# One launch of attention, a dense layer and routed experts: the first pair's keys and queries in two parts, and the experts' partial products added on VectorE

## The chip, the cores and the metric

The kernel runs on one core of one Trainium2 chip, in one launch. Its metric is the device time of the launch in microseconds (us). Before the change three runs took 764.28, 765.04 and 766.53 us; the median is 765.04. The engines are called as in the profile: PE (TensorE, matrix products; PEld its weight loads), DVE (VectorE), ACT (ScalarE), POOL (GpSimd) and SP (the engine that issues most DMAs here).

## What is computed

```python
# q, k, v: 4 batches x 8 heads x 576 positions x 64
scores = q @ k.T / 8, where block(i) >= block(j) (blocks of 64 positions), else -1e9
attn   = softmax(scores) @ v                       # -> x: 2304 tokens x 512
g      = x @ w_in;  x = max(0.01 * g, g) @ w_out   # 512 -> 2048 -> 512, all tokens
do     = x @ w_skip > 0                            # the others keep x
e      = argmax(x[do] @ w_gate), p = its softmax   # one of 8 experts for a token
out    = x + p * (relu(x @ w1[e]) @ w2[e])         # 512 -> 1024 -> 512
```

All data are 32-bit floats. A plain 32-bit product on PE (scores, expert units) is recorded as two instructions, so the profile counts twice the products of the program. In the dense layer and the first expert the operands are split in a high and a low half, and three products are made of them.

## The kernel before, in words

**Attention** goes through 16 pairs of heads. For a pair, `load` issues the DMAs of keys (`kn`), queries (`qn`) and values (`vn`) in natural layout; `prep` transposes keys and queries on PE (L110, and L160 for the first pair), ACT copies the keys to `kT` (L149), DVE and ACT each scale one head's queries into a block-diagonal operand (L170, L168; both are called `wbt` in the rows, since that is the memory they lie in). `s_steps` makes the scores of nine blocks of 64 queries, both heads in one product (L182): 64 columns for block 0, 128 for block 1, up to 576. For every block DVE takes the maximum (L192, `stat`), ACT the exponential with its sum (L193), POOL multiplies by the reciprocal (L201); then PE transposes the weights (L288) and multiplies by the values (L345). Later pairs make the scores of two blocks at a time in another form, whose mask lies in constant operands that `constants` writes once (L85 zeroes, L88 entries; tiles `wbt` and `qc`). PE reads the first of them at 88.5 us.

**The dense layer** is L526 on PE. A quarter of its first product runs between the attention steps; the rest follows, 12 chunks of 128 columns for each of 6 parts of 384 tokens. In a chunk PE makes `ph` (12 products of 384 columns), ACT and DVE make the leaky maximum `u` (L516; L517 on DVE, which lets PE reuse the bank), and PE adds 9 products of 512 columns to `acc`. DVE adds the finished sums to the tokens (L902).

**Routing.** When a part of tokens is finished, its steps wait in a list `rq`, and one is taken per chunk. For four of the six parts DVE makes the logits: nine instructions of 128x512 for a tile of 128 tokens, one step per tile (L748, `xlast`; each has a short instruction that reads the accumulator). Their place among the `u` is the scheduler's.

**Experts.** The first expert runs as full tiles. What is left is done in units: five `Groups` of up to 3, 3, 3, 1 and 1 groups of 32 tokens, one `Half` of 64, one `Full` of 128. For a group, four products that use 32 columns of PE each stand side by side. `second_product` (L1283) gives four partial sums of 32x512, one in each quarter of a bank `pp`; ACT or DVE copies them (L1394, L1358), PE adds them by a product with a matrix of ones and zeros (`py`, L1399, L1362), and DVE adds gate times result to the tokens (L1291), which POOL scatters (L1292). POOL's gather and the transposes of the next unit (L1259) and its first product (L1269, L1274) are put between.

What is written out by hand has a due time (`steps` returns pairs of time and step), and a list scheduler orders the instructions of each engine; `pin` keeps an instruction where it is written. SP issues its DMAs in its own order.

Of the kernel before, what the change touches and what calls it, by code (L numbers as in the profile page):

```python
# [10 lines left out]
F32 = mybir.dt.float32  # L11
# [16 lines left out]
class Attention:  # L28
# [50 lines left out]
    def constants(self, i):  # L79

        nc, nt, o = self.nc, self.nt, self.operands[i]
        for t, c0, val, eng in (([o["kc"][:, h] for h in range(2)], 64, self.MASK, nc.vector), (o["qc"], 0, 1.0, nc.gpsimd)):
            for h in range(2):
# [4 lines left out]
                nc.vector.tensor_scalar(out=b, in0=row, scalar1=val, scalar2=None, op0=ALU.mult)  # L88

    def load(self, p, which):  # L90
# [8 lines left out]
        for t, src in todo:  # L99
            queue = nc.scalar if p == 0 and src is self.q else nc.sync  # L100
            for j in range(2):
                queue.dma_start(t[:, 0:n, j], src[b, h0 + j, 0 : n * 128].rearrange("(t p) d -> p t d", p=128))
            queue.dma_start(t[0:64, n], src[b, h0 : h0 + 2, n * 128 : S].rearrange("h p d -> p h d"))
# [36 lines left out]
    def prep(self, p, nat):  # L140
# [9 lines left out]

        def s_q():
            if p:
                parts = [(self.transposes(qn), 0, S)]
            else:
                f = qn.rearrange("p t h d -> p t (h d)")
                parts = []
                for i0, i1 in ((0, 512), (512, S)):
                    pt = self.ps.tile([128, 512], F32, name="pq", tag="mm", bufs=2)
                    for t in range(i0 // 128, -(-i1 // 128)):
                        nc.tensor.transpose(pt[:, 128 * t - i0 : 128 * t - i0 + 128], f[:, t], self.ident)  # L160
                    parts.append((pt[:, 0 : i1 - i0], i0, i1))
            sc = self.D ** -0.5
            for pt, i0, i1 in parts:
                for h in range(2):
                    r = slice(64 * h, 64 * h + 64)
                    o, i_ = qd[r, i0 // 64 : i1 // 64, r], pt[r].rearrange("p (i c) -> p i c", c=64)
                    if h:
                        nc.scalar.activation(out=o, in_=i_, func=AF.Copy, scale=sc)  # L168
                    else:
                        nc.vector.tensor_scalar(out=o, in0=i_, scalar1=sc, scalar2=None, op0=ALU.mult)  # L170

        return st, [s_k, s_q]
# [182 lines left out]
    def steps(self, dst, lag, second):  # L355
# [16 lines left out]
        out.append((0.2, lambda: self.load(0, "v")))  # L372
        for p in range(pairs):
            t = 2 * p
            st = lambda p=p: sts[p]["st"]
            for i in range(2):
                out.append((t - ((0.9, 0.6), (1.4, 1.0))[p > self.SPLIT][i] if p else -1, lambda p=p, i=i: prep(p, i)))
            if p + 1 < pairs:
                out.append((t + lag if p else 0.6, lambda p=p: self.load(p + 1, "v")))
# [18 lines left out]
def attention_moe_kernel(  # L398
# [89 lines left out]
    def weights_a(parts, times):  # L488
# [22 lines left out]
        return [(-0.5, lambda j=j: fetch(j)) for j in range(2)] + [  # L511
# [213 lines left out]
    def routing_steps(n, x2):  # L725
# [16 lines left out]
        def logits(t):  # L742

            if t == 0:
                box["L"] = s3("lg", 1 + E)
            for j in range(1 + E):
# [106 lines left out]
        return [keep] + [lambda t=t: (logits_last if late else logits)(t) for t in range(TB)] + [route, place_all, put]  # L853
# [234 lines left out]
    for i in range(len(seq) + lag):  # L1088
# [8 lines left out]
        for _ in range(1 if i < len(seq) - NFB else 2):  # L1097
            if rq:
                rq.pop(0)()
# [177 lines left out]
    def second_product(pp, w, h, m):  # L1277

        s = 128 // m
        n = NF2 // s  # L1280
        for i in range(n):
            for j in range(s):
                pin(nc.tensor.matmul(pp[j * m : j * m + m], h[:, i * 128 + j * m : i * 128 + j * m + m], w[1][j * n + i], start=(i == 0), stop=(i == n - 1)))  # L1283

    def end_tile(y, lx, n=128):
        yo = M3.tile([128, 512], F32, name="yo")
# [226 lines left out]
```

## Time and profile before

| what | value |
|---|---|
| median of three runs | 765.04 us |
| the profiled execution | 765.64 us |
| its span, first to last instruction | 763.80 us |
| outside the span | 1.84 us |
| PE busy | 730.6 us (96%) |
| DVE, ACT, POOL busy | 460.4, 354.9, 319.2 us |
| PE idle and waiting for the first keys | 5.0 us |

The span is what the timeline shows, from 0 to 763.80; the launch's time has 1.84 us more, which no view resolves. A busy share is an average over stages: DVE is busy 60% of the span, but 49.90 of the 50 us from 450 to 500. The attention lasts to about 310 us, the dense layer to about 640 us, the units of the experts run from 682 us on.

### The profile page before, as it was taken

How to read it: one execution, taken by the hardware profiler on the slowest of the kernel's cores; microseconds unless marked ns; L12 is line 12 of the kernel's file. 1: busy time of each engine (PE TensorE's matmuls, PEld its weight loads, DVE VectorE, ACT ScalarE, POOL GpSimd, SP SyncE). 2: the span in 40 equal slices, each digit the busy share in tenths (PEclk: the TensorE clock that was granted, in tenths of full speed). 3: DMA queues.
4: the chain of work that ended last, by engine and by line, in shares of the span. 5: the costliest groups of instructions: out<-in, count | busy, mean ns of one | idle time of the engine just before them, and what ended most of it. 6: DMA issues, size and time to landing. Idle time of an engine off the chain costs nothing.

```text
span 763.8 us, 12641 instructions
## 1 busy us (share of the span) xinstructions
PE 730.6 (96%) x4454; PEld 593.1 (78%) x4455; DVE 460.4 (60%) x1067; ACT 354.9 (46%) x824; POOL 319.2 (42%) x429
## 2 busy tenths in 40 slices
PE   5999899999999999999999999999999998999995
PEld 4666778788888788899999998879899976875333
DVE  5888887764668646666773499988821365221211
ACT  4786887775788746555452222222223251222110
POOL 4656683454335436454442342545431543210111
PEclk9999999999999999999999999999999999999998
DMA  8545644522330214732223457112302221999900
GB/s 183 136 116 133 181 103 113 144 65 73 90 77 17 95 58 148 272 100 81 98 83 111 123 150 251 56 43 84 125 0 83 57 96 32 301 399 397 353 25 24
DMA packets 101109, 96.92 MB, mean 127 GB/s; under 512 B 69198, under 2 KB 72270, under 8 KB 101042
## 3 DMA queue, kind: packets, MB, share of 16 engines
q1 hardware_dynamic: 92578, 82.28, 34.5%
q0 software_dynamic: 7264, 13.50, 6.1%
q8 instruction: 36, 0.59, 0.3%
q10 hardware_dynamic: 1200, 0.30, 0.2%
q14 instruction: 31, 0.25, 0.1%
HBM read 74.38 MB, written 21.98 MB: 126 GB/s over the span
## 4 chain that ended last, share of the span: by engine, by line
PE 64%; DVE 21%; ACT 7%; DMA 3%; issue 2%; POOL 1%; SPq 0%; POOLq 0%; ACTq 0%; DVEq 0%
PE ph L526 18%; PE acc L526 12%; DVE xlast L748 9%; PE pv L345 4%; PE po L526 3%; PE ph L1269 3%; PE pp L1283 3%; PE pt L288 3%; PE py L1004 2%; PE sp L229 2%; PE ph L1004 2%; ACT P L193 2%; PE sp L182 2%; DVE stat L192 2%; PE big L110 1%
## 5 line engine op out<-in xcount | busy, mean ns | idle before, releaser
L526 PE MATMUL ph<-xT,wbt 128*128 128x384 f32 x864 | 167.2, 338 | 3.9 <-DVE u L517 2.1
L526 PEld LDWEIGHTS ph<-xT,wbt 128*128 128x128 f32 x864 | 151.8, 188 | 13.5 <-DVE u L517 3.9
L518 POOL TENSOR_TENSOR gl<-u,gh 128x384 fp32r<-128x384 f32 x72 | 80.5, 1119 | 144.5 <-ACT gh L517 140.8
L526 PE MATMUL acc<-wbt,gh 128*128 128x512 f32 x432 | 132.2, 393 | 0.0
L201 POOL TENSOR_SCALAR P<-P,stat 128x256 f32<-128x256 f32 (+4 forms) x144 | 80.0, 573 | 89.5 <-DVE stat L199 73.3
L517 ACT CAST gh<-u 128x384 fp32r<-128x384 f32 x72 | 37.0, 514 | 121.2 <-DVE u L517 49.6
L526 PEld LDWEIGHTS acc<-wbt,gh 128*128 128x128 f32 x432 | 79.7, 188 | 12.0
L517 DVE TENSOR_TENSOR u<-ph,u 128x384 f32<-128x384 f32 x72 | 39.7, 551 | 71.4 <-ACT u L516 71.3
L526 PE MATMUL acc<-wbt,gl 128*128 128x512 f32 x216 | 82.2, 395 | 0.0
L516 ACT ACTIVATE u<-ph 128x384 f32<-128x384 f32 x72 | 35.3, 490 | 61.3 <-PE ph L526 58.2
L288 PE MATMUL pt<-ident,P 128*128 128x128 f32 x400 | 58.2, 275 | 4.4 <-ACT P L193 1.8
L192 DVE TENSOR_REDUCE stat<-sp 128x1 f32<-128x384 f32 (+7 forms) x88 | 45.9, 527 | 25.1 <-PE sp L229 12.8
L288 PEld LDWEIGHTS pt<-ident,P 128*128 128x128 f32 x400 | 47.0, 140 | 16.5 <-ACT P L193 5.4
L193 ACT ACTIVATE P<-sp,stat 128x384 f32<-128x384 f32 (+7 forms) x88 | 49.8, 567 | 20.2 <-DVE stat L192 18.6
L526 PE MATMUL ph<-xT,wia 128*128 128x384 f32 x288 | 57.6, 344 | 0.6 <-ACT xT L350 0.5
L473 POOL TENSOR_TENSOR cv<-cv,cv 128x512 int32<-128x512 int32 x32 | 43.7, 1366 | 33.7 <-DVE cv L472 26.9
L526 PE MATMUL po<-woa,gA 128*128 128x512 f32 x216 | 55.4, 399 | 0.0
L748 DVE CUSTOM_DVE_ANT_0 xlast<-x,raw 128x512 f32<-128x512 f32 x72 | 55.1, 804 | 0.0
L526 PEld LDWEIGHTS ph<-xT,wia 128*128 128x128 f32 x288 | 49.4, 188 | 2.3 <-ACT xT L350 0.7
L345 PE MATMUL pv<-ph,vn 128*64 128x320 f32 (+4 forms) x448 | 49.6, 370 | 0.4 <-ACT P L242 0.3
L526 PEld LDWEIGHTS acc<-wbt,gl 128*128 128x128 f32 x216 | 40.4, 188 | 8.5
L345 PEld LDWEIGHTS pv<-ph,vn 128*64 128x64 f32 x448 | 30.3, 140 | 20.8 <-issue 2.8
(282 smaller groups left out, 1249.6 us busy)
## 6 DMA issues: line engine op xcount, KB each, us to landing
wbt<-in_moe_w_dram SPq DMA_DIRECT2D x40, 512.0 KB
raw<-in_moe_w_in_dram SPq DMA_DIRECT2D x16, 512.0 KB
raw<-in_moe_w_out_dram SPq DMA_DIRECT2D x16, 512.0 KB
xTd<-xT POOLq DMA_DIRECT2D x4, 1152.0 KB
part_d<-cv SPq DMA_DIRECT2D x18, 256.0 KB
x<-part_d SPq DMA_DIRECT2D x6, 768.0 KB
xT<-xTd POOLq DMA_DIRECT2D x6, 768.0 KB
out_dram<-x SPq DMA_DIRECT2D x6, 768.0 KB
```

Source lines behind the costliest of these rows:

```text
L192: self.recent["max"] = nc.vector.tensor_reduce(out=st_[:, 1, i : i + 1], in_=sv, op=ALU.max, axis=ax, negate=True)
L193: self.recent["exp"] = nc.scalar.activation(out=P, in_=sv, func=AF.Exp, bias=st_[:, 1, i : i + 1], accum_out=st_[:, 0, i : i + 1])
L201: nc.gpsimd.tensor_scalar(out=P, in0=P, scalar1=rs[:, i : i + 1], scalar2=1.0, op0=ALU.mult, op1=ALU.mult)
L288: nc.tensor.transpose(o, src, self.ident)
L345: self.pin(nc.tensor.matmul(box["pv"][64 * h : 64 * h + 64, c0:N], st()["vs"][:, jc, h], box["ph"][:, i, h, cs], start=(jc == 0), stop=(jc ...
L473: nc.gpsimd.tensor_tensor(out=w, in0=w, in1=low, op=ALU.add)
L516: nc.scalar.activation(out=u, in_=ph, func=AF.Copy, scale=0.01)
L517: return [nc.vector.tensor_tensor(out=u, in0=ph, in1=u, op=ALU.max), nc.scalar.copy(gh, u), nc.gpsimd.tensor_tensor(out=gl, in0=u, in1=gh. ...
L518: nc.gpsimd.tensor_tensor(out=gl, in0=u, in1=gh.bitcast(F32), op=ALU.subtract)]
L526: nc.tensor.matmul(ps, x, y, start=first and m == 0, stop=last and m == 3 * n - 1)
L748: nc.vector.tensor_tensor_reduce(out=junk, in0=x2[:, t], in1=wrow[j], scale=1.0, scalar=0.0, op0=ALU.mult, op1=ALU.add, accum_out=box["L"] ...
L1004: nc.tensor.matmul(ps, x, y, start=(i == 0), stop=(i == len(l) - 1))) for i, (x, y) in enumerate(l)]
```

## The change

Six things change.

1. The first pair's keys and queries are loaded and prepared in two parts: positions 0 to 255, then 256 to 575. The scores of blocks 0 to 3 need only the first part and stand between. The second part is due at 0.41 and not at -1.
2. The second pair's queries are transposed into the banks `mm`, in parts, and not into the bank pair `big`.
3. `constants(0)` is written by POOL alone: three zeroings and four tensor_scalar leave DVE. `constants(1)` stays as it was, with the entries of its tile `qc` written by DVE.
4. The values' loads of the first three pairs are pinned, and due later; so are the first fetches of the dense weights (0.6 and not -0.5).
5. The logits of a tile are made in two steps of 5 and 4 instructions, `keep` goes with the first, and a step of `rq` is issued behind the maximum `u` of its chunk.
6. `second_product` makes partial sums of 256 columns, in the same number of quarters: two quarters hold the two halves of the columns for one half of the hidden units, two for the other. DVE adds the four straight from the bank, with gate and token (`add_groups`). The copies, the products with ones and the matrices for them are gone.

```diff
-        for t, c0, val, eng in ((... self.MASK, nc.vector), (o["qc"], 0, 1.0, nc.gpsimd)):
+        engines = (nc.gpsimd, nc.gpsimd) if i == 0 else (nc.vector, nc.gpsimd)
+        for t, c0, val, eng in ((... self.MASK, engines[0]), (o["qc"], 0, 1.0, engines[1])):
                 eng.memset(t[h][r].bitcast(F32), 0.0)
...
-                nc.vector.tensor_scalar(out=b, in0=row, scalar1=val, scalar2=None, op0=ALU.mult)
+                engines[0].tensor_scalar(out=b, in0=row, scalar1=val, scalar2=1.0, op0=ALU.mult, op1=ALU.mult)
...
+        cuts = ((0, 2), (2, n)) if p == 0 and which != "v" else ((0, n),)
+        pin = self.pin if p < 3 and which == "v" else lambda ins: ins
...
+                queue = nc.scalar if a < e < n and src is self.q else nc.sync
...
+        def both(i0, i1):
+            pt = self.ps.tile([128, 512], F32, name="pk", tag="ps", bufs=4)
+            f = kn.rearrange("p t h d -> p t (h d)")
+            for t in range(i0 // 128, -(-i1 // 128)):
+                nc.tensor.transpose(pt[:, 128 * t - i0 : 128 * t - i0 + 128], f[:, t], self.ident)
+            a = part(qn, i0, i1)
+            nc.scalar.copy(kT[:, i0:i1], pt[:, 0 : i1 - i0])
+            put_q(*a)
+
+        if p == 0:
+            return st, [lambda: both(0, 256), lambda: both(256, S)]
...
-                out.append((... if p else -1, lambda p=p, i=i: prep(p, i)))
+                out.append((... if p else (-1, 0.41)[i], lambda p=p, i=i: prep(p, i)))
...
             if rq:
-                rq.pop(0)()
+                with tc.issue_after(ends[0].ins):
+                    rq.pop(0)()
...
+            turns = [lambda t=t, js=js: logits(t, js) for t in range(TB) for js in (range(0, 5), range(5, 1 + E))]
...
     def second_product(pp, w, h, m):
         s = 128 // m
         n = NF2 // s
-        for i in range(n):
+        for i in range(2 * NF2 // s):
             for j in range(s):
-                pin(nc.tensor.matmul(pp[j * m : j * m + m], h[:, i * 128 + j * m : ...], w[1][j * n + i], ...))
+                f = j // 2 * 4 + i
+                c, d = f % n * 128 + f // n * m, j % 2 * 256
+                pin(nc.tensor.matmul(pp[j * m : j * m + m, 0:256], h[:, c : c + m], w[1][f][:, d : d + 256], ...))
...
+    def add_groups(yo, pp, lx, t0, m):
+        r = slice(t0, t0 + m)
+        for j in range(128 // m):
+            c = slice(j % 2 * 256, j % 2 * 256 + 256)
+            nc.vector.scalar_tensor_tensor(out=yo[r, c], in0=pp[j * m : j * m + m, 0:256], scalar=lx["li"][r, 2:3], in1=(lx["xg"], yo)[j // 2][r, c], op0=ALU.mult, op1=ALU.add)
...
                 second_product(pp, self.w, hT[:, g // 2, g % 2 * 256 : g % 2 * 256 + 256], MG)
-                (nc.vector.tensor_copy if g % 2 else nc.scalar.copy)(ev[g], pp)
+                add_groups(self.yo, pp, self.lx, g * MG, MG)
...
-            y = psx.tile([128, 512], F32, name="py", bufs=1)
-            for g in range(self.n // MG):
-                pin(nc.tensor.matmul(y[g * MG : g * MG + MG], sums[MG], ev[g], start=True, stop=True))
-            end_tile(y, self.lx, self.n)
+            end_tile(self.yo, self.lx, self.n)
```

The order of the instructions on an engine is shown at three places: rows before, then rows now. Line numbers of the changed kernel are some lines higher (L110 is L116, L182 is L200, L192 is L210, L748 is L767, L1283 is L1310).

First, the start of DVE. Before, the zeroes of the first operand, then all constants, then the queries, then the first maxima:

```order
L57 MEMSET wbt_89 64x9x64 x2
L85 MEMSET wbt_88 64x576 x2
L88 TENSOR_SCALAR wbt_88<-ident 64x4x64 x3
L88 TENSOR_SCALAR qc_107<-ident 64x4x64
L88 TENSOR_SCALAR qc_108<-ident 64x4x64
L170 TENSOR_SCALAR wbt_89<-pq 64x8x64
L170 TENSOR_SCALAR wbt_89<-pq 64x64
L192 TENSOR_REDUCE stat<-sp 128x1 x5
```

Now, the same engine from the same row on:

```order
L57 MEMSET wbt_89 64x9x64 x2
L172 TENSOR_SCALAR wbt_89<-pq 64x4x64
L89 TENSOR_SCALAR qc_108<-ident 64x4x64
L210 TENSOR_REDUCE stat<-sp 128x1 x4
L172 TENSOR_SCALAR wbt_89<-pq 64x5x64
L216 TENSOR_SCALAR stat<-stat 128x4
L217 RECIPROCAL stat<-stat 128x4
L210 TENSOR_REDUCE stat<-sp 128x1 x2
```

The constants of the first set have left DVE; one instruction that writes entries of the second set's `qc` tile, which waits for POOL's zeroes of that tile, stands between the first part's queries and the first maximum.

At the same place, ACT before, from its first copy on:

```order
L149 COPY wbt_89<-big 128x576
L168 ACTIVATE wbt_89<-pq 64x8x64
L168 ACTIVATE wbt_89<-pq 64x64
L193 ACTIVATE P_109,stat<-sp,stat 128x64
L193 ACTIVATE P_109,stat<-sp,stat 128x128
L193 ACTIVATE P_109,stat<-sp,stat 128x256
L193 ACTIVATE P_109,stat<-sp,stat 128x192
L193 ACTIVATE P_109,stat<-sp,stat 128x320
L149 COPY wbt_89<-big 128x576
L193 ACTIVATE P_109,stat<-sp,stat 128x384
```

And ACT now:

```order
L185 COPY wbt_89<-pk 128x256
L170 ACTIVATE wbt_89<-pq 64x4x64
L211 ACTIVATE P_109,stat<-sp,stat 128x64
L211 ACTIVATE P_109,stat<-sp,stat 128x128
L211 ACTIVATE P_109,stat<-sp,stat 128x256
L185 COPY wbt_89<-pk 128x320
L211 ACTIVATE P_109,stat<-sp,stat 128x192
L170 ACTIVATE wbt_89<-pq 64x5x64
L211 ACTIVATE P_109,stat<-sp,stat 128x320
L211 ACTIVATE P_109,stat<-sp,stat 128x384
```

The second part's copy of the keys and scaling of the queries stand among the first exponentials, behind the third and behind the fourth.

Second, DVE in the dense layer while it makes logits (with the buffers' numbers). Before, the rows that lead up to one `u`, in the profile at 465.74 to 469.17 us:

```order
L748 ISA lg_5057 128x1
L789 TENSOR_TENSOR ohb_4888<-oh_4886,go_4884 128x24
L814 RECIPROCAL li_4933<-sm_4935 128x3
L748 ISA xlast_5108,lg_5057<-x2_3719,raw_4416 128x512
L748 ISA lg_5057 128x1
L748 ISA xlast_5110,lg_5057<-x2_3719,raw_4416 128x512
L748 ISA lg_5057 128x1
L748 ISA xlast_5112,lg_5057<-x2_3719,raw_4418 128x512
L748 ISA lg_5057 128x1
L748 ISA xlast_5114,lg_5057<-x2_3719,raw_4418 128x512
L748 ISA lg_5057 128x1
L517 TENSOR_TENSOR u_5018<-ph2_5003,u_5018 128x384
```

Now, the rows from one `u` to the next:

```order
L535 TENSOR_TENSOR u_5091<-ph2_5076,u_5091 128x384
L767 ISA xlast_5099,lg_5098<-x2_3728,raw_4425 128x512
L767 ISA lg_5098 128x1
L767 ISA xlast_5101,lg_5098<-x2_3728,raw_4425 128x512
L767 ISA lg_5098 128x1
L767 ISA xlast_5103,lg_5098<-x2_3728,raw_4427 128x512
L767 ISA lg_5098 128x1
L767 ISA xlast_5105,lg_5098<-x2_3728,raw_4427 128x512
L767 ISA lg_5098 128x1
L767 ISA xlast_5107,lg_5098<-x2_3728,raw_4429 128x512
L767 ISA lg_5098 128x1
L535 TENSOR_TENSOR u_5133<-ph2_5118,u_5133 128x384
```

Every step of five or four logits stands behind a `u`, and small routing instructions no longer lie between them here.

Third, PE in the experts, from the second product of the first unit to that of the second. Before:

```order
L1283 MATMUL pp<-wbt_6887,raw 32x512 x24
L1269 MATMUL ph_7389<-wbt_7194,cv_6924 32x256 x16
L1274 MATMUL pt<-ident,cv_7214 128x128 x4
L1274 MATMUL pt<-ident,cv_7215 128x128 x2
L1269 MATMUL ph_7417<-wbt_7194,cv_6924 32x256 x16
L1269 MATMUL ph_7435<-wbt_7194,cv_6924 32x256 x16
L1399 MATMUL py<-raw,sum_7220 32x512 x3
L1259 MATMUL pt<-ident,xgf_3562 128x32 x4
L1283 MATMUL pp<-wbt_6897,raw 32x512 x24
```

Now:

```order
L1310 MATMUL pp<-wbt_6896,raw 32x256 x48
L1293 MATMUL ph_7426<-wbt_7203,cv_6933 32x256 x16
L1298 MATMUL pt<-ident,cv_7223 128x128 x4
L1298 MATMUL pt<-ident,cv_7224 128x128 x2
L1293 MATMUL ph_7454<-wbt_7203,cv_6933 32x256 x16
L1293 MATMUL ph_7472<-wbt_7203,cv_6933 32x256 x16
L1283 MATMUL pt<-ident,xgf_3571 128x32 x4
L1310 MATMUL pp<-wbt_6906,raw 32x256 x48
```

The products with ones (L1399) are gone; the second product has twice the instructions at half the columns.

## Rows read from the trace of the kernel before

**Rows 1.** The page: busy time by engine, and the chain's shares
```profile
PE 730.6 (96%) x4454; PEld 593.1 (78%) x4455; DVE 460.4 (60%) x1067; ACT 354.9 (46%) x824; POOL 319.2 (42%) x429
...
PE 64%; DVE 21%; ACT 7%; DMA 3%; issue 2%; POOL 1%; SPq 0%; POOLq 0%; ACTq 0%; DVEq 0%
```

**Rows 2.** Waits of PE: us in total, times, longest
```profile
PE big L110 <- DMA kn<-in_k_dram: 5.0, 1, 5.0
PE sp L229 <- ACT ph L290: 2.6, 4, 1.2
PE ph L526 <- DVE u L517: 2.1, 3, 0.8
...
PE big L182 <- ACT wbt L168: 1.7, 1, 1.7
```

**Rows 3.** Timeline of the start: start, duration, engine, line, count, [idle before]
```profile
4.98 1.08 PE L110 MATMUL big<-ident,kn 128*128 128x128 f32 x4 [4.98 <-DMA kn<-in_k_dram]
5.24 0.74 DVE L88 TENSOR_SCALAR wbt<-ident 64x256 fp32r<-64x256 f32 x1 [0.70 <-POOL wbt L85]
5.26 1.24 POOL L85 MEMSET qc<- 64x576 f32 x2
...
6.96 0.81 DVE L170 TENSOR_SCALAR wbt<-pq 64x512 f32<-64x512 f32 x2
...
7.84 0.70 ACT L168 ACTIVATE wbt<-pq 64x512 f32<-64x512 f32 x2
...
8.48 5.06 PE L182 MATMUL sp<-wbt 128*128 128x64 f32 x12 [1.13 <-ACT wbt L168]
...
10.38 0.23 DVE L192 TENSOR_REDUCE stat<-sp 128x1 f32<-128x64 f32 x1 [2.60 <-PE sp L182]
...
16.06 0.71 PE L110 MATMUL big<-ident,qn 128*128 128x128 f32 x5
...
17.79 0.65 ACT L168 ACTIVATE wbt<-big 64x576 f32<-64x576 f32 x1
18.49 1.24 PE L182 MATMUL big<-wbt 128*128 128x288 f32 x4 [1.72 <-ACT wbt L168]
```

**Rows 4.** Windows: stretch, then PE, PEld, DVE, ACT, POOL, granted clock
```profile
90.00:93.00 3.00, 1.46 (x10) 0.79 (x10) 2.88 (x7) 2.67 (x8) 2.33 (x3) 1.00 0.26 58
93.00:96.40 3.40, 3.40 (x18) 1.88 (x20) 3.32 (x8) 1.70 (x6) 1.90 (x3) 0.50 0.00 0
```

**Rows 5.** Timeline of the dense layer at 468.5, and a window around it
```profile
468.28 0.62 PE L526 MATMUL acc<-wbt,gh 128*128 128x512 f32 x2
...
468.55 0.68 DVE L748 CUSTOM_DVE_ANT_0 xlast<-x,raw 128x512 f32<-128x512 f32 x1
468.75 0.40 PE L526 MATMUL acc<-wbt,gl 128*128 128x512 f32 x1
...
469.17 0.55 DVE L517 TENSOR_TENSOR u<-ph,u 128x384 f32<-128x384 f32 x1
...
469.77 2.39 PE L526 MATMUL ph<-xT,wbt 128*128 128x384 f32 x12 [0.62 <-DVE u L517]
...
450.00:500.00 50.00, 48.99 (x260) 43.27 (x259) 49.90 (x148) 10.59 (x24) 20.66 (x19) 1.00 0.39 127
```

**Rows 6.** Timeline of the experts' units
```profile
694.46 5.36 PE L1283 MATMUL pp<-wbt,raw 128*32 128x512 f32 x48
...
702.28 3.66 PE L1269 MATMUL ph<-wbt,cv 128*32 128x256 f32 x64
...
705.75 1.03 PE L1399 MATMUL py<-raw,sum 128*32 128x512 f32 x6
...
706.72 0.43 PE L1259 MATMUL pt<-ident,xgf 32*128 32x32 f32 x4
...
706.90 0.75 DVE L1291 SCALAR_TENSOR_TENSOR yo<-py,rankli,xg 96x512 f32<-96x512 f32 x1 [3.71 <-PE py L1399]
...
752.23 0.48 DVE L1291 SCALAR_TENSOR_TENSOR yo<-py,rankli,xg 128x256 f32<-128x256 f32 x1 [2.91 <-PE py L1336]
```

More of the change, by code (lines that the diff above doesn't have):

```diff
@@ L149, in s_k, with part @@
             nc.scalar.copy(kT, self.transposes(kn))
-        def s_q():
[L152 to L170, printed above, removed]
+        def part(nat, i0, i1):
+            f = nat.rearrange("p t h d -> p t (h d)")
+            pt = self.ps.tile([128, 512], F32, name="pq", tag="mm", bufs=2)
+            for t in range(i0 // 128, -(-i1 // 128)):
+                nc.tensor.transpose(pt[:, 128 * t - i0 : 128 * t - i0 + 128], f[:, t], self.ident)
+            return pt[:, 0 : i1 - i0], i0, i1
@@ new lines, in put_q @@
+        def put_q(pt, i0, i1):
+            sc = self.D ** -0.5
+            for h in range(2):
+                r = slice(64 * h, 64 * h + 64)
+                o, i_ = qd[r, i0 // 64 : i1 // 64, r], pt[r].rearrange("p (i c) -> p i c", c=64)
+                if h:
+                    nc.scalar.activation(out=o, in_=i_, func=AF.Copy, scale=sc)
+                else:
+                    nc.vector.tensor_scalar(out=o, in0=i_, scalar1=sc, scalar2=None, op0=ALU.mult)
+        def s_q():
+            parts = [(self.transposes(qn), 0, S)] if p > 1 else [part(qn, i0, i1) for i0, i1 in ((0, 512), (512, S))]
+            for a in parts:
+                put_q(*a)
@@ L740, in keep, with logits @@
             tc.keep_in_program_order(nc.sync.dma_start(out[rows].rearrange("(t p) d -> p t d", p=128), x2))
-        def logits(t):
-            if t == 0:
+        def logits(t, js):
+            if t == 0 and js[0] == 0:
+                keep()
                 box["L"] = s3("lg", 1 + E)
-            for j in range(1 + E):
+            for j in js:
                 junk = M2.tile([128, D], F32, name="xlast", bufs=3)
@@ L852, in routing_steps @@
             return dict(keep=keep, turn=turn_last, mul=mul_last, route=route, rank=rank, place=place_all, put=put)
-        return [keep] + [lambda t=t: (logits_last if late else logits)(t) for t in range(TB)] + [route, place_all, put]
+        if late:
+            turns = [keep] + [lambda t=t: logits_last(t) for t in range(TB)]
+        else:
+            turns = [lambda t=t, js=js: logits(t, js) for t in range(TB) for js in (range(0, 5), range(5, 1 + E))]
+        return turns + [route, place_all, put]
     parts = {}
@@ L1339, in end @@
         def end(self):
-            end_tile(self.y, self.lx, self.n)
+            yo, lx = out_tile(), self.lx
+            for k_, y in enumerate(self.y):
+                c = slice(k_ * 256, k_ * 256 + 256)
+                nc.vector.scalar_tensor_tensor(out=yo[:, c], in0=y, scalar=lx["li"][:, 2:3], in1=lx["xg"][:, c], op0=ALU.mult, op1=ALU.add)
+            end_tile(yo, lx)
     class Half(Unit):
@@ L1357, in second @@
             second_product(pp, self.w, hT[:, 0], MH)
[L1358 removed]
+            self.yo = out_tile()
+            add_groups(self.yo, pp, self.lx, 0, MH)
         def end(self):
[L1361 to L1363 removed]
+            end_tile(self.yo, self.lx, MH)
     class Groups(Unit):
@@ L1419, in attention_moe_kernel @@
     h2 = [CV.tile([128, 512], F32, name="cv3", bufs=3) for _ in range(2)]
-    hT, ev01, ev23 = (CV.tile([128, 2, 512], F32, name="raw", bufs=3) for _ in range(3))
-    ev = [ev01[:, 0], ev01[:, 1], ev23[:, 0], ev23[:, 1]]
+    hT = CV.tile([128, 2, 512], F32, name="raw", bufs=3)
     hx = CV.tile([128, 512], F32, name="cv2", bufs=3)
-    sums = {m: M3.tile([128, m], F32, name=f"sum{m}", bufs=1) for m in (MG, MH)}
-    for m, t in sums.items():
-        nc.vector.reduce_sum(out=t, in_=ident.rearrange("p (s t) -> p t s", t=m), axis=AX.X)
     units[0].first()
@@ L1469, in half @@
         second_product(pp, w, hT[:, 1], MH)
-        nc.scalar.copy(hx, pp)
-        y = bank("py")
-        pin(nc.tensor.matmul(y[0:MH], sums[MH], hx, start=True, stop=True))
-        end_tile(y, lx, MH)
+        yo = out_tile()
+        add_groups(yo, pp, lx, 0, MH)
+        end_tile(yo, lx, MH)
     with tc.If(spill > 0):
```

40 lines of the change are left out of this document (18 added, 22 removed).

## Prediction, made before the changed kernel ran

> **What bounds the kernel now.** I read the page first: PE is busy 96% of the span and makes most of the chain that ended last [rows 1]. The reader should see that no other engine is near its limit on the average, so that a gain must come from PE work that goes or from PE waits. The waits of PE come next [rows 2]: one of 5.0 us for the first keys, small ones on ACT and DVE in the attention, 2.1 us on the maximum `u`. Then I read the timeline at the three places that the change touches: the start [rows 3], the dense layer while DVE makes logits [rows 5], the experts' units [rows 6]. The window around the second place shows DVE busy 49.90 of 50 us, so there PE waits for a full engine, which the page's 60% hides. A last view is the granted clock [rows 4].
>
> The sum is made against the profiled execution, 765.64 us (span 763.80 and 1.84 outside it). The median of the runs, 765.04, is 0.60 lower; I take that off at the end.
>
> **The experts' units.** The sum products go. In the first unit they start at 705.75 and the next transposes at 706.72 [rows 6]: 0.97 us of PE, and nothing waits there, so it is path. The profile repeats this step five times, one per `Groups` unit, also where there is one group: 5 x 0.97 = 4.85 us. The twelve copies of the banks run on ACT and DVE beside PE and give nothing. The second product grows: 24 products of 512 columns, 5.36 us, become 48 of 256. The first product has that very shape, 64 records or 32 products in 3.66 us [rows 6], 0.114 each; 48 make 5.49, or 0.13 more in each of three large units, and about 0.15 more in the small ones and the `Half` together: +0.5.
>
> New is DVE. A row of the same operation, 128x256, takes 0.48 us [rows 6]. A group needs four: 1.92 if each waits for the one before it to end, against 1.83 of PE for 16 products. In a unit of three groups DVE starts when the first group's bank is complete, 3.66 before PE ends the third, and does 12 x 0.48 = 5.76: it ends 2.1 us after PE. Behind these adds stand the copies of the next hidden units, which PE needs for its next second product. After the first unit PE has 16 + 32 products and transposes to do, over 5 us of work by 0.114 each, and sees nothing. After the second it has 16 products (1.83), six transposes and four small ones (about 1.3 by 0.71 for five [rows 3] and 0.43 [rows 6]): 3.1 us, against 2.1 and two copies of about 1.0 in all. That is even; I take 0.1, with 0 to 0.5 as bounds. Nothing else in the tail changes: the `Half` loses its sum product but puts two adds in front of the copies that PE waits for, which I count as nothing, give or take 0.3. So -4.85 + 0.5 + 0.1 = -4.25; bounds -4.9 and -3.5.
>
> Two DVE instructions in a row overlap in the dense layer: one that takes 0.68 is followed 0.62 later [rows 5]. If adds overlapped likewise, they would go at 0.42 and the 0.1 would be 0. [...]
>
> **The logits.** At 468.75 PE begins the last product before its `ph`; two such products record 0.62 and one 0.40, so the next could start 0.22 later, but `ph` starts at 469.77, since `u` ran only at 469.17, behind four logits in a row [rows 5]. That lost 0.80. The pattern stands four times between 450 and 550 us; by starts they lose 3.1, by the idle rows 2.1 [rows 2]. The reordered DVE has `u` before each step: 0.55 and five logits, 0.62 apart, make 3.65 us. A chunk on PE is 21 products, and the window has 260 in 50 us: about 4.0. Where the three sums `x` of a finished part, of like size, fall in the same chunk, four logits and these make 4.9, which overruns that chunk by 0.9; the next regains 0.4. So I take the waits as gone but for a remainder: -2.6, between 2.1 and 3.1, and what is late next is nothing on DVE. The logits take two chunks for a tile instead of one, but the lists that hang on them are needed far behind. The least that this edit can bring is 0, if the sums stand wrongly in every part.
>
> **The start.** PE waits until 4.98 for 576 keys and queries; the first part is under half of the bytes, so it can be there between 2.5 (if the whole time scaled) and 4.98. I take 3.8, the middle. Four transposes of two tensors take half as long as eight, about 1.0 at the pace of 1.08 for four [rows 3]; then DVE and ACT scale 256 columns, about 0.4 each, where 512 took 0.7 to 0.8. So scores start at 5.1 to 5.9, not at 8.48. The first maximum came 1.90 after that and would come at 7.0 to 7.8. But the row in front of it now waits for POOL's zeroes of `qc`, which ended at 6.50 and now have two more zeroings of 0.62 in front of them: 7.7, and then up to 0.74 for the row itself, less if nothing disturbs it [rows 3]. The maximum comes at 8.0 to 8.4, against 10.38: -2.2. It is not all kept. ACT now has a copy of 320 columns and a scaling of 320 (0.4 to 0.5 each) among the exponentials, which before lay ahead of them, and one instruction more for the second pair: about 1.2 of the 2.2 goes. ACT's order paces PE here, since the second pair's scores wait for ACT's scaling at 17.79 and start at 18.49 [rows 3]. I take -0.9, with -2.2 (all kept) and +1.0 as bounds; the latter if block 4, whose operands now stand behind three exponentials, comes a microsecond later than before and everything behind it. POOL's four tensor_scalar cost nothing: POOL has nothing else to do from there until the first exponentials are multiplied, and the constants are read only by later pairs. On SP's queue the values' loads now follow the second pair's keys and queries and two weight fetches; they are first used when weights have been transposed, behind the second pair's scores, so I count nothing.
>
> **The clock.** In the first stretch products take twice as long as later: four transposes 1.08, later five 0.71 [rows 3]. [...]
>
> **The sum.** -4.25 - 2.6 - 0.9 = -7.75: 757.9 by the profiled execution, 757.3 as a median.
>
> **Rivals.**
> (a) The start brings nothing or loses: PE's idle stretch between block 3 and block 4 grows from nothing to over 2 us, and the second pair starts no earlier than at 18.49. For it: one row that waits for POOL, and ACT's new order; against it: 2.2 us of head start. The other terms stay: 765.04 - 6.85 = 758.2, and with the bound of +1.0, 759.2. [...]
> (b) The waits on `u` only move: two of four stay. 758.6; if all stay, 759.9. For it: DVE is as full as before (49.90 of 50); against it: the even spacing.
> (c) More is gained: the start keeps its 2.2 and the waits before the clock's fall at 93 dissolve with the new phase: 757.3 - 1.3 - 1.7 = 754.3.
> (d) DVE becomes the bound in the units: if an add of 256 columns cost 0.75, what one of 512 takes [rows 6], 12 of them make 9.0 and end 5.3 behind PE; the second unit's hidden units come 3.1 late and the third's about 2. That gives back 5: 762.3.
> (e) Slower: the attention's new phase brings further falls of the clock. PE's order differs in the first pairs, which shifts the later ones, and each wait of PE like the one at 90 to 93 can be followed by a stretch at 0.50, at 1.7 us. It decides from the fifth fall on (757.3 + 8.5 = 765.8); with seven it is 769. For it: one such fall is there and PE waits on ACT in several places; against it: one fall in 16 pairs.
>
> **How the numbers follow.** Chances: forecast (755.5 to 759 by its own bounds) 0.50, (a) 0.18, (b) 0.10, (c) 0.11, (d) 0.06, (e) 0.05. A measurement of this kernel can tell about 0.3% from no change, 2.3 us. All of the first four and most of (d) lie under 762.7, so faster has 0.89; (d) with a little more, or a mixture of (a), (b) and (d), gives 0.06 for no change; (e) 0.05 for slower. The range leaves out (e), half of (d) and the far part of (c): 753.5 to 761.5.
>
> **What would show it.** PE's first transposes at 3.5 to 4; DVE's first maximum at 8.0 to 8.4 and, in front of it, a wait for POOL; the second pair's first scores at 17 to 18. No wait of PE on `u` above 0.2 between 450 and 550. In the units, transposes that follow the first product without 0.97 between them, adds of 0.48, and a wait on DVE's copies of the hidden units only in front of the third second product. I am wrong in kind if the tail from the first unit to the end is not 3.5 to 4.9 shorter, if adds take much over 0.5, or if the granted clock falls in more places than one.

## The result, and the profile after

The changed kernel takes 756.29 us, the median of five runs from 754.77 to 756.97; the kernel before, beside it, took 764.36. The ratio is 0.9884, 95% interval 0.9867 to 0.9902. The forecast was 757.3, the range 753.5 to 761.5. The profiled execution has a span of 754.5 us, 9.3 less than before.

The page's rows on busy time and on the chain, which answer to [rows 1]:

```profile
PE 721.1 (96%) x4622; PEld 597.0 (79%) x4623; DVE 472.6 (63%) x1097; ACT 351.0 (47%) x817; POOL 322.6 (43%) x435
...
PE 79%; DVE 8%; ACT 6%; DMA 3%; issue 2%; POOL 1%; POOLq 0%; SPq 0%; ACTq 0%; DVEq 0%
```

DVE had 21% of the chain and has 8: a wait on DVE has left the path, though DVE is busier than before. The waits of PE (us in total, times, longest), which answer to [rows 2], say which one:

```profile
PE pk L183 <- DMA kn<-in_k_dram: 3.7, 1, 3.7
...
PE po L544 <- DVE xT L369: 1.6, 1, 1.6
...
PE big L116 <- DMA kn<-in_k_dram: 1.5, 1, 1.5
...
PE pp L1310 <- DVE raw L1299: 0.9, 2, 0.5
```

The wait on `u` is not there any more; three new rows are. To see what each place gave, I set the start of every matrix product against that of the same product before. PE is 2.7 us ahead where the attention ends, 6.9 after the logits, 5.3 behind the first expert, and 9.2 at the end. So the start and the attention gave 2.7, the logits 4.2, something took 1.5 at the first expert, and the units gave 3.9, of it 0.45 in front of their first second product. The runs below show that the third of these numbers is the clock, and that the first is there only where the clock does not fall near 23 us. The 0.45 is no gain of the new units: PE starts the first second product as much earlier in start_only, logits_only and logits_place, which have the units of before.

**The start**, in rows that answer to [rows 3]:

```profile
3.67 0.66 PE L183 MATMUL pk<-ident,kn 128*128 128x128 f32 x2 [3.67 <-DMA kn<-in_k_dram]
...
5.67 2.71 PE L200 MATMUL sp<-wbt 128*128 128x64 f32 x8 [0.92 <-ACT wbt L170]
6.32 1.09 POOL L86 MEMSET qc<- 64x576 f32 x2
7.45 0.28 DVE L89 TENSOR_SCALAR qc<-ident 64x256 fp32r<-64x256 f32 x1 [2.24 <-POOL qc L86]
...
7.66 0.21 DVE L210 TENSOR_REDUCE stat<-sp 128x1 f32<-128x64 f32 x1
...
8.18 0.85 PE L183 MATMUL pk<-ident,kn 128*128 128x128 f32 x3
...
8.84 0.92 SPq L107 DMA_DIRECT2D kn<-in_k_dram  x2
...
10.81 3.06 PE L200 MATMUL sp<-wbt 128*128 128x320 f32 x8 [1.24 <-ACT wbt L170]
...
15.83 1.24 PE L200 MATMUL big<-wbt 128*128 128x288 f32 x4 [0.22 <-ACT wbt L155]
...
18.59 1.09 SPq L107 DMA_DIRECT2D kn<-in_k_dram  x2
...
22.05 0.63 PE L116 MATMUL big<-ident,kn 128*128 128x128 f32 x4 [1.48 <-DMA kn<-in_k_dram]
```

The scores begin 2.8 us earlier, the first maximum 2.7, the first pair's last block (`big`) 2.7. At 22.05 most of this head start is gone: PE waits 1.48 for the third pair's keys. Before, SP issued them at 15.54 and PE transposed them at 21.45. The first products with values start at 29.89, before at 30.24; by 84 us PE is again 2.0 ahead (v_late below says more).

The third pair's keys are late because the second pair's are. Before, SP issued these at 6.10:

```profile
6.10 0.92 SPq L102 DMA_DIRECT2D kn<-in_k_dram  x2
```

Now it waits until 8.84, since the second part of the first pair's keys, which is transposed from 8.18 on, still fills the buffer that they go to. From the second pair's keys to the third's SP takes 9.4 us before and 9.8 now, with six DMAs of values between them in both.

**The logits.** The window that [rows 5] has for before, and PE around one `u`:

```profile
450.00:500.00 50.00, 50.00 (x260) 45.09 (x259) 39.39 (x114) 12.43 (x26) 21.72 (x20) 1.00 0.41 127
```
```profile
470.52 0.56 DVE L535 TENSOR_TENSOR u<-ph,u 128x384 f32<-128x384 f32 x1 [3.64 <-ACT u L534]
...
471.59 0.39 PE L544 MATMUL acc<-wbt,gl 128*128 128x512 f32 x1
...
471.82 2.25 PE L544 MATMUL ph<-xT,wbt 128*128 128x384 f32 x12
```

The last product before `ph` starts at 471.59 and `ph` 0.23 later, since `u` ran at 470.52. PE is busy in all of the window, and DVE in 39.39 us of 50 where it was in 49.90: the same logits are spread over more time.

**The units**, in rows that answer to [rows 6]:

```profile
700.47 5.39 PE L1310 MATMUL pp<-wbt,raw 128*32 128x256 f32 x96
...
705.68 1.04 PE L1293 MATMUL ph<-xT,cv 128*32 128x256 f32 x16
...
706.56 0.99 DVE L1316 SCALAR_TENSOR_TENSOR yo<-pp,rankli,xg 32x256 f32<-32x256 f32 x2
...
707.58 1.00 DVE L1316 SCALAR_TENSOR_TENSOR yo<-pp,rankli,yo 32x256 f32<-32x256 f32 x2
...
708.61 1.02 DVE L1299 COPY raw<-pt 128x512 f32<-128x512 f32 x2
...
709.36 5.39 PE L1310 MATMUL pp<-wbt,raw 128*32 128x256 f32 x96 [0.47 <-DVE raw L1299]
...
717.84 1.93 PE L1310 MATMUL pp<-xT,raw 128*32 128x256 f32 x32 [0.47 <-DVE raw L1299]
```

The adds take 0.47 to 0.49 and go 0.51 apart; those of the second unit end 2.9 us after its last product (708.58 against 705.68), the copies stand behind them, and PE waits in front of the third and of the fourth second product.

**The clock** (window, busy time of PE, PEld, DVE, ACT, POOL, then the granted clock), which answers to [rows 4]; the first row is where it had fallen before, the second is where it falls now:

```profile
93.00:96.40 3.40, 3.40 (x30) 3.24 (x27) 3.29 (x8) 1.78 (x5) 2.37 (x3) 1.00 0.00 0
...
623.80:627.10 3.30, 3.30 (x11) 2.20 (x10) 1.26 (x11) 0.22 (x1) 0.00 (x0) 0.50 0.01 4
```

It stays up at 93 and falls at 623.8, for 3.4 us as before; PE had waited 1.4 us for tokens at 616. The fall at 623.8 took 1.5 at the first expert. That the one at 93 is gone gave nothing that lasts: PE's lead over the kernel before grows from 2.0 to 3.9 us between 92 and 97, and is back at 2.2 by 150. The new wait for `xT` among the waits of PE above is part of this. The run late_adds3 below has the same instructions in the same order on PE up to there, and its clock does fall at 89.9. That puts it 1.3 us behind the changed kernel at 97, but it does not wait for `xT` and starts the products behind that wait 0.2 ahead (changed kernel first, then late_adds3):

```profile
99.71 0.47 PE L544 MATMUL po<-woa,gA 128*128 128x512 f32 x1 [1.56 <-DVE xT L369]
```
```profile
99.53 0.70 PE L544 MATMUL po<-woa,gA 128*128 128x512 f32 x2
```

### The profile page after: what moved, and what is told of

Same layout as the page of the kernel before. It is cut to its first block, busy times and chain, and to the rows that moved or that the text cites. A ratio compares the mean times of both kernels' runs of the same rounds, so it can differ in the third digit from the quotient of the medians.

```text
span 754.5 us, 13003 instructions
## 1 busy us (share of the span) xinstructions
PE 721.1 (96%) x4622; PEld 597.0 (79%) x4623; DVE 472.6 (63%) x1097; ACT 351.0 (47%) x817; POOL 322.6 (43%) x435
## 4 chain that ended last, share of the span: by engine, by line
PE 79%; DVE 8%; ACT 6%; DMA 3%; issue 2%; POOL 1%; POOLq 0%; SPq 0%; ACTq 0%; DVEq 0%
PE ph L544 25%; PE acc L544 19%; PE pv L363 4%; PE po L544 3%; PE pt L306 3%; PE pp L1310 3%; PE ph L1293 3%; PE sp L247 2%; PE py L1027 2%; PE ph L1027 2%; PE sp L200 2%; ACT P L211 2%; DVE stat L210 1%; PE big L116 1%; PE big L247 1%
## 5 line engine op out<-in xcount | busy, mean ns | idle before, releaser
L544 PE MATMUL ph<-xT,wbt 128*128 128x384 f32 x864 | 165.5, 337 | 1.0 <-ACT cv L592 1.0
L536 POOL TENSOR_TENSOR gl<-u,gh 128x384 fp32r<-128x384 f32 x72 | 83.5, 1162 | 135.8 <-ACT gh L535 123.6
L210 DVE TENSOR_REDUCE stat<-sp 128x1 f32<-128x384 f32 (+7 forms) x88 | 46.1, 528 | 24.4 <-PE sp L247 15.0
L767 DVE CUSTOM_DVE_ANT_0 xlast<-x,raw 128x512 f32<-128x512 f32 x72 | 51.6, 764 | 0.0
L363 PE MATMUL pv<-ph,vn 128*64 128x320 f32 (+4 forms) x448 | 47.7, 361 | 0.1
L544 PEld LDWEIGHTS po<-woa,gA 128*128 128x128 f32 x216 | 39.4, 188 | 9.8 <-issue 1.9
```

The costliest lines, as they stand in the source:

```text
L210: self.recent["max"] = nc.vector.tensor_reduce(out=st_[:, 1, i : i + 1], in_=sv, op=ALU.max, axis=ax, negate=True)
L363: self.pin(nc.tensor.matmul(box["pv"][64 * h : 64 * h + 64, c0:N], st()["vs"][:, jc, h], box["ph"][:, i, h, cs], start=(jc == 0), stop=(jc ...
L536: nc.gpsimd.tensor_tensor(out=gl, in0=u, in1=gh.bitcast(F32), op=ALU.subtract)]
L544: nc.tensor.matmul(ps, x, y, start=first and m == 0, stop=last and m == 3 * n - 1)
L767: nc.vector.tensor_tensor_reduce(out=junk, in0=x2[:, t], in1=wrow[j], scale=1.0, scalar=0.0, op0=ALU.mult, op1=ALU.add, accum_out=box["L"] ...
```

## The experiments

Each ran with the kernel before on the same chip.

| run | what it is | median us | ratio to before, 95% |
|---|---|---|---|
| tail_only | before + adds on DVE | 761.15 | 0.9945 [0.9929, 0.9962] |
| logits_only | before + two steps, bound behind `u` | 761.72 | 0.9951 [0.9932, 0.9970] |
| start_only | before + the rest | 764.67 | 0.9992 [0.9982, 1.0002] |
| logits_split | before + two steps, not bound | 765.35 | 0.9999 [0.9986, 1.0012] |
| logits_place | before + bound, nine in a step | 762.10 | 0.9958 [0.9944, 0.9971] |
| consts_dve | changed, constants by DVE | 757.86 | 0.9898 [0.9875, 0.9922] |
| v_late | changed, values later | 758.21 | 0.9901 [0.9874, 0.9929] |
| late_adds | changed, last adds moved | 757.70 | 0.9897 [0.9870, 0.9924] |
| late_adds2 | the same, bound | 757.04 | 0.9880 [0.9858, 0.9903] |
| late_adds3 | late_adds2, a free buffer | 754.61 | 0.9869 [0.9852, 0.9885] |
| all_late | late_adds3 and v_late | 756.19 | 0.9881 [0.9862, 0.9900] |
| after_again | the changed kernel | 756.57 | 0.9897 [0.9879, 0.9916] |

**The three parts apart.** Their edits are the hunks of the diff above: `second_product` to `end_tile` (tail_only); `logits`, the list of turns and `issue_after` (logits_only); all others (start_only).

> The kernel before with the new second product and the adds on DVE alone. Theory (the parts add up, each in its own place): from the first unit to the end 3.5 us less, as between the two traces (five sum products at 0.85 to 0.98 gone, two stalls of 0.55 before the third and fourth second product come), everything ahead of the units as before, the fall of the granted clock at 93 us too; total -3.5. Rival (the tail's gain depends on the phase that the earlier parts give it, through the weights' arrival): the 0.45 in front of the first second product is missing or more of the stalls come, total outside -3.0 to -4.0. My recorded sum was -4.25.

> The kernel before with the logits in two steps behind the maximum u alone. Theory: all waits of PE on u between 450 and 550 us go, -4.2 by 600 us as between the two traces, more than the 2.6 of my sum, because the idle rows leave out part of what the waits cost; the clock's fall at 93 stays where it was, and none comes at 623; total -4.2. Rival one, my recorded sum: -2.6. Rival two, the fall of the clock goes with the wait before the first expert at 617 us and comes in any case when the logits are earlier: total -2.7 with a stretch at 0.50 near 619.

> The kernel before with the start alone: two parts, the second queries in other banks, constants by POOL, later values' loads. Theory: -2.3 by 20 us, and -2.7 by 310 us, of which about 1.7 is the fall of the clock at 93 that does not come there; total -2.7, or -1.0 where the fall comes in another place. Rival, my recorded sum: -0.9 with the fall at 93 where it was.

They add up: 0.55 + 0.49 + 0.08 = 1.12% against 1.16% and 1.03% for the whole in two measurements. The tail alone shortens the units by 3.5 us in the trace from their first second product on, as expected, and 0.4 more goes in front of it, as in start_only, whose units are those of before; nothing earlier moves but the start, which is 0.7 ahead of the profile of before with the same instructions. The logits alone give 4.2 between 440 and 600 us, so my recorded 2.6 falls. In that execution the clock falls at 91, at 135 and at 627, each of the last two for 1.5, and the trace ends 2.8 ahead, near rival two; the median of its runs is 3.4 below the kernel before. The start alone gives 0.6, at most 1.4 by its interval, and perhaps nothing. Its trace shows where the rest goes:

```profile
19.00:22.50 3.50, 1.61 (x10) 0.90 (x9) 1.91 (x9) 3.01 (x10) 2.45 (x5) 1.00 0.79 165
22.70:26.00 3.30, 3.30 (x9) 1.85 (x8) 1.32 (x3) 2.11 (x6) 0.89 (x3) 0.50 0.79 206
```

PE is busy 1.61 us of 3.5, since it waits 1.43 for the third pair's keys, and behind that the clock falls to 0.50. At 40 us PE is no longer ahead of the kernel before, and at 400 us 0.95. The changed kernel, without that fall, is 2.7 ahead there. A second fall, at 630, takes 1.5 more, so that in this execution the start ends with nothing.

**Split or place.** What of the logits' edit does it?

```diff
 # logits_split: two steps, as in the change, but
-                with tc.issue_after(ends[0].ins):
-                    rq.pop(0)()
+                rq.pop(0)()
 # logits_place: issue_after kept, nine logits in a step as before
```

> The kernel before with the logits in two steps but not bound behind the maximum u. Theory (what removes the waits is that a u comes after at most five logits, for which the scheduler needs the binding): some waits stay, PE gains 1 to 3 of the 4.2 us between 450 and 600. Rival one (the split alone does it): 4.2. Rival two (the binding alone does it): within 0.5 of nothing.

> The kernel before with each routing step bound behind the maximum u of its chunk, but nine logits in a step as before. Theory (both are needed: nine logits of 0.61 and u make 6.0 us, longer than a chunk): PE still waits on u, at most half of the 4.2 us comes, or it is slower than before. Rival (the binding alone does it, since logits_split alone did nothing): 3.5 to 4.2 by 600 us.

Waits of PE on `u`, logits_split first, then logits_place:

```profile
PE ph L526 <- DVE u L517: 1.6, 3, 0.6
```
```profile
PE ph L526 <- DVE u L517: 0.7, 1, 0.7
```

The split alone does nothing; the binding alone gives 3.35 of the 4.2 us by 600 us, more than the half that I allowed. So the place behind `u` is the cause, and by the traces shorter steps add the last 0.8; the runs' intervals overlap. My theory that both are needed falls.

**The constants.** `engines = (nc.vector, nc.gpsimd)` for both sets, as before.

> The changed kernel with the mask constants written by DVE as before, the two parts kept. Theory (the constants in front of the queries hold the first scores, which is why they had to leave DVE): the first part's queries are scaled at 5.8 to 6.3 and not at 4.8, the first maximum at 8.6 to 9 and not at 7.66, total up to 1.0 slower. Rival (PE gives the head start back in any case): the first maximum comes late and PE at 150 us is where it was within 0.3.

```profile
6.00 0.42 DVE L172 TENSOR_SCALAR wbt<-pq 64x256 f32<-64x256 f32 x1
...
6.88 2.71 PE L200 MATMUL sp<-wbt 128*128 128x64 f32 x8 [2.15 <-ACT wbt L170]
...
8.78 0.22 DVE L210 TENSOR_REDUCE stat<-sp 128x1 f32<-128x64 f32 x1 [1.84 <-PE sp L200]
```

The first maximum comes 1.1 us later, and PE is 1.0 behind the changed kernel until 90 us; at 150 it is 0.3 behind. The place is as expected; of the price most is given back, and the intervals of the two overlap. The run also sizes the row in front of the first maximum: here nothing holds the maximum, and it comes 1.90 behind the first score. In the changed kernel that would be 7.57; it comes at 7.66. The hold costs 0.1.

**The values' loads.** In the changed kernel six DMAs of values (13.51 to 18.49 us) stand on SP's queue in front of the third pair's keys, as six did before (10.82 to 15.44).

```diff
-        out.append((0.75, lambda: self.load(0, "v")))
+        out.append((1.5, lambda: self.load(0, "v")))
-                out.append((t + lag if p else 1.0, ...
+                out.append((t + lag if p else 1.6, ...
```

> The changed kernel with the first two pairs' values loaded behind the third pair's keys and queries on SP's queue, not in front. Theory (the head start of the start is given back at 20.6 us, where PE waits 1.48 for the third pair's keys, since six DMAs of values stand in front of them on SP's queue): that wait goes, and PE is 1.5 us ahead of the changed kernel at 25 us. How much of it is left at 150 us is open: all of it if PE bounds the first pairs, less than 0.5 if ACT and DVE do. Rival: the keys wait for their buffer, which PE's transposes free, and come at the same time: the wait stays.

```profile
10.87 4.70 PE L200 MATMUL sp<-wbt 128*128 128x320 f32 x8 [1.08 <-ACT wbt L170]
...
20.48 0.71 PE L116 MATMUL big<-ident,kn 128*128 128x128 f32 x5
...
31.05 0.74 PE L116 MATMUL big<-ident,kn 128*128 128x128 f32 x5 [1.06 <-DMA kn<-in_k_dram]
```

SP now issues the keys at 16.04, and PE transposes them at 20.48 without a wait. That the values stood in the way is shown. But the time is not lower: the values now stand in front of the fourth pair's keys, which SP issues at 25.62 for 24.68, and PE waits 1.06 for them at 30 us, as much as it had gained (against late_adds below, whose first 20 us are as slow, it starts the products with values at 29.12 for 30.18). And from 24 us on PE's order in v_late is that of the kernel before, over which its lead stays at 0.8 us. In the changed kernel the scheduler has put PE in another order, with the third pair's keys transposed later, and there the lead grows from 0.35 at 30 us to 2.0 at 84: PE is idle for 1.0 us in that stretch, before for 1.9 and in v_late for 2.3. The clock falls at 92.7, which costs nothing here either: against all_late below, with PE in the same order and no such fall, v_late is 0.4 ahead at 90 us, 1.3 behind at 97 and 0.3 ahead at 120. And a thing that no order explains: the eight products at 10.87, the same as those at 10.81 in the changed kernel, take 4.70 and not 3.06, the first five of them 3.46 for 1.83.

**The adds of a last group.** Besides what is shown, `turn_groups` keeps its copy in `turned[0]`.

```diff
...
+                if g == self.n // MG - 1:
+                    self.late = pp
+                else:
                     add_groups(self.yo, pp, self.lx, g * MG, MG)
...
         def end(self):
+            with tc.issue_after(turned[0].ins):      # late_adds: without this line
+                add_groups(self.yo, self.late, self.lx, self.n - MG, MG)
...
 # late_adds3 besides: the last unit's rows
-            self.lx = lane32(RL, li, xgs[(i + 1) % 4], xws[i % 3])
+            self.lx = lane32(RL, li, xgs[4 if i == 6 else (i + 1) % 4], xws[i % 3])
```

> The changed kernel, with the adds of a unit's last group issued in front of the scatter, so behind the copies of the next hidden units on DVE. Theory (the stalls before the third and fourth second product are DVE's copies that queue behind the adds, 12 adds at 0.51 against 5.39 of PE): both waits of 0.47 go, -1.0 against the changed kernel. Rival (the stall is the copies' own length, 1.02, behind the transposes): the waits stay and the time does not move beyond 0.3 us; or the last bank is held longer and PE waits for a bank instead.

> The changed kernel with the adds of a unit's last group bound behind the copies of the next hidden units; the run late_adds left the order of DVE as it was, this one has the copies in front. Theory: both waits of 0.47 before the third and fourth second product go and nothing takes their place: the stretch from the first unit's second product to the end is 1.0 us shorter than in the changed kernel. Rival: the copies start when their transposes end and are 1.02 long, so 0.2 to 0.5 of each wait stays: 0.2 to 0.6 shorter.

> The run late_adds2 with the last unit's gathered rows in a buffer that is free early. Theory (what gave back the 1.1 us of late_adds2 was the gather of the last unit, which waits until DVE has read the buffer for the unit three before it): the wait of 1.19 at that unit's transposes goes too, and from the first second product to the end it is 1.1 us shorter than the changed kernel. Rival: the gather waits for something else on POOL's queue and the wait stays.

late_adds tells nothing of the stall: the scheduler put the adds where they had been, and it is the changed kernel once more. With the binding (late_adds2) both waits of 0.47 go and PE gains 1.1 us by 720; then it waits for the last unit's rows and is 0.2 behind where it began:

```profile
716.48 0.99 POOL L735 DMA_INDIRECT xg<-x_d,rankix  x1 [5.78 <-PE pp L1312]
...
722.53 0.63 PE L1283 MATMUL pt<-ident,xg 128*128 128x128 f32 x4 [1.19 <-DMA xg<-x_d,rankix]
```

With a buffer that is free early (late_adds3) the gather goes ahead and the wait is gone:

```profile
719.46 1.94 PE L1293 MATMUL ph<-wbt,cv 128*64 128x512 f32 x8
...
721.33 0.66 PE L1283 MATMUL pt<-ident,xg 128*128 128x128 f32 x4
```

From the first second product to the end it is 1.08 shorter than the changed kernel, as the theory said. Its runs, 753.82 to 755.98, all lie under those of after_again beside it, 756.17 to 759.18, but two of the changed kernel's first five, 754.77 and 754.85, lie among them, and the intervals overlap. It has the lowest median here; shown is the 1.08 in the trace.

**All together, and the changed kernel once more.**

> late_adds3 and v_late together: adds of a last group behind the copies, last unit's rows in a free buffer, first two pairs' values behind the third pair's keys. Theory: the idle time of PE adds up, 1.1 less in the units and 2.6 less before 150 us than in the changed kernel, so 1 to 3.5 us faster in runs with as many stretches at 0.50. Rival: as in v_late, the time is not below the changed kernel's, since more stretches at 0.50 come.

> The changed kernel once more, beside the next two. Theory (the difference between its own runs, 754.8 to 757.0, is stretches of 3.41 us at a granted clock of 0.50 that come in one execution and not in another, 1.5 to 1.7 us each): the runs again lie in groups by their mean clock, about 754.8 at 0.996 and 756.5 to 757 at 0.994 or 0.993, and the profile's stretch stands at another place or is not there. Rival: the stretch belongs to the order of the work, and stands at 623 us again in each.

all_late is not faster than late_adds3: the later values bring nothing that lasts. As in v_late, PE has the order of the kernel before from 24 us on and waits for the fourth pair's keys (1.29 at 31 us); it starts the first products with values 0.5 ahead of late_adds3 and is 1.7 behind it at 90 us. In after_again, with the same instructions in the same order, the clock's stretch at 0.50 stands at 22.8 and not at 623.8:

```profile
22.90:26.20 3.30, 3.30 (x11) 2.18 (x10) 1.32 (x3) 1.74 (x6) 1.03 (x3) 0.50 0.72 197
...
623.80:627.10 3.30, 3.30 (x22) 2.97 (x22) 3.01 (x15) 0.23 (x1) 0.00 (x0) 1.00 0.19 70
```

It goes from 0.35 to 2.1 behind the first profile there, is 1.8 behind at 600 and catches up 1.5 at 623.8. So the place of a stretch is not fixed by the order. The order bears on it all the same: with the start as before all five profiles have a fall at 91 to 93, with the new start two of nine (v_late, late_adds3); with the logits bound behind `u` seven of ten have one at 624 to 628, without one of four (start_only, at 630). The groups by mean clock, which I had expected, are loose: runs at 0.995 take from 754.8 to 757.3.

## Why the prediction held, point by point

The time came out within 1.0 us. The three terms were -4.25, -2.6 and -0.9. Between the two profiles the units give -3.45 from their first second product on and -0.45 in front of it, the logits -4.2, the start and the attention -2.7, and a fall of the clock that I did not count takes 1.5: -9.3 in all, where the medians differ by 8.1. The kinds were right. That the sum held is partly luck: the logits and, in this execution, the start gave more than forecast, the units less, and the clock took back 1.5.

**Units.** Right in kind. The five sum products gave 0.85 to 0.98 each, 4.5 in all, not 4.85; the second product grew by 0.03 a unit, not 0.13. The term that was mis-sized is the adds' stall, taken as 0.1: it measured 1.1. "12 x 0.48" left out that the first add begins 0.18 behind its bank and that they go 0.51 apart, so that DVE ends 2.9 and not 2.1 behind PE; and the fourth second product, which I counted as nothing, waits too. late_adds2 and late_adds3 take this wait away and so show its cause. By my own sign of being wrong, 3.5 to 4.9 from the first unit to the end, the tail lies at the edge: 3.9 with the 0.45 in front, 3.45 without. The adds do not overlap: one of 0.47 to 0.49 is followed 0.51 later, not 0.42, where logits of 0.68 follow each other 0.61 apart; what makes the difference, no run shows. Rival (d) thus came in part, 1.1 of its 5 us.

**Logits.** Right in place and cause, too small in size: 4.2 for 2.6. Summing the idle rows (2.1) or the four late starts (3.1) leaves out about a microsecond that PE loses in steps too short for an idle row; which steps, is open. The sentence that DVE would be "as full as before" was wrong: it is busy 39 of 50 us. Rival (b) did not come.

**Start.** The first steps held: transposes at 3.67 for 3.8, scores at 5.67 for 5.1 to 5.9. (The lower bound for the keys, 2.5 "if the whole time scaled", is 2.2 for 256 of 576 positions.) The first maximum came at 7.66, not at 8.0 to 8.4, since POOL's zeroes end at 7.41 and the held row takes 0.28. I misread one row: the products at 18.49 are the last block of the first pair, which waited until ACT's scaling freed the bank `big`; the change of banks for the second queries removes that wait, and the block comes at 15.83. At 20 us PE was 2.3 ahead.

The step that failed is "so I count nothing" on SP's queue. I followed the values there and not the buffer of the keys: the second pair's keys wait for the first pair's second part and are issued 2.7 later than before, and all that SP issues behind them is late too, so PE waits 1.48 for the third pair's keys. v_late shows that with fewer values in front of them this wait goes, that the next keys then bring one of 1.06, and that PE then has the order of before, in which its lead does not grow. ACT's order, to which I gave the loss, takes part of it at 10.81, where PE waits 1.24.

How much the start is worth hangs on the clock. At 400 us PE's lead is 2.7 in the changed kernel's profile, and 0.9 in after_again and start_only, where the clock falls behind the wait at 22 us. Nor is the start of before fixed: tail_only, logits_split and logits_place, which have it, are 0.3 to 0.7 ahead of the profile of before there. The ten runs of start_only give 0.6; their interval holds my 0.9 and also rival (a), that the start brings nothing.

**Clock.** The sum counts nothing for the granted clock, and that was wrong. Rivals (c) and (e) price a fall at 1.7 wherever it stands, an estimate: half of the 3.4 us at 0.50 in [rows 4]. No run shows 1.7. At 22.8 (after_again) a fall cost 1.75, at 623.8 1.5, and both stayed; at 89.9 (late_adds3) it cost 1.45, all given back at the wait for `xT`. v_late beside all_late says the same for the order of before. So the fall at 93 that went was worth nothing, where (c) counts 1.7 for it, and the one at 623.8 that came cost 1.5. The wait of 1.2 at 90 us did not dissolve; rival (e), that the new order brings falls elsewhere, came in kind. The falls at 22.8, 93.0 and 623.8 came behind waits of PE of 1.55, 1.22 and 1.41 us. But behind the wait at 22 us the clock fell in two executions (after_again, start_only) and not in three (the changed kernel's first, consts_dve, late_adds2), and the fall at 135 in logits_only came behind no wait above 0.7. What sets a fall is not shown.

## What to carry to other kernels

Where a full engine serves another at fixed points, bind the filler work behind each serving instruction: here the place gave most of the gain, and smaller pieces alone gave nothing. When work leaves a path, look for the next thing that queues behind what replaced it, first on its engine and then in the buffers that it holds longer, as the adds, then the gather. A load moved "later" is moved in front of something on its queue; look who, and look which buffer each load waits for. What a slow stretch of an engine costs depended here on whether that engine waited for another soon behind it: of PE's stretches at 0.50 two cost 1.75 and 1.5 us for good, and one of 1.45 was given back at a wait.

## What the runs showed of the hardware

The granted clock falls to 0.50 in stretches of 3.4 us. Such a stretch cost 1.75 us for good at 22.8 (after_again), 1.5 at 623.8 (the changed kernel's first profile), and nothing at 89.9 (late_adds3), since PE in an execution without that fall waits 1.56 for DVE ten us later. Between none (late_adds2) and three (logits_only) of them came in the profiled executions ahead of the kernel's end, at 23, 90 to 93, 135 and 624 to 630 us. Their place moves between executions of one and the same order (623.8 and 22.8), so a single profile of each of two kernels can differ by the 1.5 to 1.75 of one stretch at a place that the change does not touch. The end of the slow pace at the start moves as well: the same eight products took 3.06 us in five of the nine profiles with the new start and 4.59 to 5.01 in the other four. By 25 us this is evened out where the third pair's keys come late: PE waits 1.48 for them in the changed kernel (3.06), 0.23 in late_adds (4.59), and the two are 0.3 apart behind that. The changed kernel's first five runs lie 2.2 us apart, so effects below about 2 us are seen product by product in the traces rather than in the total.
